# A new static order for a fused attention and feed-forward kernel, with Omega's transpose in steps, five buffers of attention outputs and constant matmuls in gaps

## Chip, cores and metric

The kernel runs on one core of one Trainium2 chip. The metric is device time in microseconds (us). Fast executions of one kernel mostly agree to within about 1% (three of the kernel before: 325.45 to 328.21 us). A run counts as slow when it is over 1.5% above the fastest of its kernel. A profiled span is some 1.7 us shorter than the time of the same run, in most runs (327.8 for 329.58 us before). The granted clock is the share of its full clock that the profile records for TensorE. In the profiles PE is TensorE, PEld its weight loads, DVE VectorE, ACT ScalarE, POOL GpSimd, SP SyncE; a q behind a name marks its instruction queue.

## What is computed

Eight batches of eight heads go through linear attention with random features. The 4608 rows that come out go through a two-layer feed-forward net.

```python
q_s, k_s = q * scale, k * scale            # q, k, v: (8, 8, 576, 64) float32
def phi(x):
    h = einsum('bhsd,md->bhsm', x, omega) - sum(x * x) / 2      # omega: (128, 64)
    return exp(h - max(h)) / sqrt(m)
kv, z = einsum('bhsm,bhsd->bhmd', phi(k_s), v), sum(phi(k_s), over s)
x = (phi(q_s) @ kv) / (phi(q_s) @ z + 1e-6)                      # -> (4608, 512)
h = x @ w_in                                                     # (512, 2048)
out = (h * sigmoid(1.702 * h)) @ w_out                           # (2048, 512), float32 out
```

## The kernel before

The work is cut into 32 attention items (item p is one pair of heads; four items are one batch) and eight blocks (one batch of 576 rows each through both layers). A block's first layer needs the attention outputs of its four items, transposed. In the steady loop from block 2 on, items of later batches are woven between the wide matmuls of the current blocks. Ahead of the loop stands a prologue: items 0 to 13, block 0's two layers, and block 1's first layer. Its steps are listed by hand, one call per step. That list is each engine's program order.

The output of an item is divided into a buffer `xb`, and a DMA transpose moves it to its place in `xt`, which the first layer reads. `xb` comes from a pool of three:

```python
work = ctx.enter_context(tc.tile_pool(name="work", bufs=3))
...
def xb_tile(p):
    if (p, "xb") not in st:
        st[p, "xb"] = work.tile([128, NCH, 128], BF16, name="xb", tag="xb")
    return st[p, "xb"]
...
def xt_dma(p):                                   # two pieces, on SyncE's queue
    xb = st.pop((p, "xb"))
    ...
    nc.sync.dma_start_transpose(dst[:, 0:512]..., xb[:, 0:4, :]...)
    nc.sync.dma_start_transpose(dst[:, 512:S], xb[64:128, 4, :])
```

The start, and two places of the hand-made list (`tk`, `tq`: PE transposes of k and q; `pk`, `pq`: projections; `e_..`: ScalarE exponentials; `halves_max`, `maxima`, `inverse`: VectorE; `scale_v`: values scaled, on GpSimd if True; `kv`, `nd`: the attention products; `mm1`, `mm2`: the wide matmuls of the two layers):

```python
warm_ps = bank("b1", [128, 512], F32, "warm_ps")
for _ in range(9):                               # constants, to bring the full clock
    nc.tensor.matmul(warm_ps[:], lhsT=warm[:, 0:128], rhs=warm[:])
...
def omega_T():
    for i in range(2):
        nc.vector.tensor_copy(out=om_b[:, 64 * i : 64 * i + 64], in_=om_f[:])
    omt_ps = bank("b1", [128, 128], BF16, "omt_ps")
    nc.tensor.transpose(omt_ps[:], om_b[:], ident[:])
    nc.vector.tensor_copy(out=omT2[:], in_=omt_ps[:])
...
    omega_T()
    load_k(0, 2, 3)
    k0_cast(False)                               # VectorE's part of the first k, behind Omega's copy
    k0_cast(True)
    tk_pe(0, "b0")
    ...                                          # cut
    xt_dma(6)
    pk_pe(9)
    ...
    nd2_pe(7, "qp")
    nd2_inv(7)
    nd2_div(7)                                   # needs a fourth xb while three wait for their transposes
    e_k5(9)
    ...
    xt_dma(7)
```

The softmax here doesn't subtract the row's maximum and nothing guards it: scores larger than these inputs give would overflow.

Of the kernel before, what the change touches and what calls it, by code (L numbers as in the profile page):

```python
# [13 lines left out]
F32 = mybir.dt.float32  # L14
# [7 lines left out]
def kernel(  # L22
# [45 lines left out]
    work = ctx.enter_context(tc.tile_pool(name="work", bufs=3))  # L68
    small = ctx.enter_context(tc.tile_pool(name="small", bufs=4))
# [19 lines left out]
    warm_ps = bank("b1", [128, 512], F32, "warm_ps")  # L89
    for _ in range(9):  # L90
        nc.tensor.matmul(warm_ps[:], lhsT=warm[:, 0:128], rhs=warm[:])  # L91
# [353 lines left out]
    def xb_tile(p):  # L445
        if (p, "xb") not in st:
            st[p, "xb"] = work.tile([128, NCH, 128], BF16, name="xb", tag="xb")
        return st[p, "xb"]
# [207 lines left out]
    om_f = const.tile([128, D], F32, name="om_f")  # L656
# [3 lines left out]
    nc.scalar.dma_start(om_f[:], omega[:, :])  # L660
# [7 lines left out]
    def omega_T():  # L668
        for i in range(2):
            nc.vector.tensor_copy(out=om_b[:, 64 * i : 64 * i + 64], in_=om_f[:])  # L670
        omt_ps = bank("b1", [128, 128], BF16, "omt_ps")
        nc.tensor.transpose(omt_ps[:], om_b[:], ident[:])
        nc.vector.tensor_copy(out=omT2[:], in_=omt_ps[:])
# [18 lines left out]
    with tc.manual_schedule(engines={ET.DVE, ET.Activation}):  # L692
        make_identity(nc, ident[:])
        omega_T()
        load_k(0, 2, 3)
        k0_cast(False)
        k0_cast(True)
        tk_pe(0, "b0")
        load_k(0, 1, 2)
        tk_cp(0, False)  # L700
        load_k(0, 3, 4)
        load_q(0, 1, 2)
        q0_cast(True)
        tk_pe(2, "b1")
        tk_cp(2, False)
        pf_pe(0)
        e_k5(0)
        load_q(0, 2, 3)
        pk_pe(0)
        e_km(0)  # L710
        tk_pe(1, "b0")
        q0_cast(False)
        tk_cp(1, False)
        tq_pe(0, "b1")
        tq_cp(0, True)
        halves_max(0)
        pf_pe(1)
        pk_pe(1)
        maxima(0)
        pq_pe(0)  # L720
        inverse(0)
        tk_pe(3, "b1")
        e_k5(1)
        tk_cp(3, False)
        tq_pe(1, "b0")
        load_v(0, 0, 1, nc.gpsimd)
        tq_cp(1, False)
        pr_pe(0)
        load_k(1, 0, 1)
        load_k(1, 1, 2)  # L730
        load_v(0, 1, 2, nc.gpsimd)
        e_km(1)
        load_k(1, 2, 3)
        halves_max(1)
        pk_pe(2)
        maxima(1)
        pf_pe(3)
        tq_pe(2, "b1")
        e_qm(0)
        pf_pe(2)  # L740
        inverse(1)
        load_v(0, 2, 4, nc.gpsimd)
        tq_cp(2, False)
        load_q(0, 3, 4)
        load_q(1, 0, 1)
        scale_v(0, True)
        pq_pe(1)
        tk_pe(4, "b0")
        e_km(2)
        pk_pe(3)  # L750
        tk_cp(4, False)
        e_k5(2)
        halves_max(2)
        kv_pe(0)
        e_qm(1)
        kv_cp(0)
        e_qr(0)
        maxima(2)
        nd_pe(0, 0, "b0")
        nd_inv(0, 0)  # L760
        load_win(0)
        e_k5(3)
        nd_pe(0, 1, "b1")
        nd_inv(0, 1)
        tk_pe(6, "qp")
        pr_pe(1)
        e_km(3)
        tk_cp(6, False)
        pr_pe(2)
        nd_div(0, 1, True)  # L770
        pf_pe(4)
        scale_v(1, True)
        halves_max(3)
        inverse(2)
        maxima(3)
        kv_pe(1)
        nd_div(0, 0, True)
        e_qr(1)
        xt_dma(0)
        load_q(1, 2, 3)  # L780
        pq_pe(2)
        e_qm(2)
        tk_pe(5, "b1")
        load_win(1)
        tk_cp(5, False)
        pk_pe(4)
        scale_v(2, True)
        e_k5(4)
        inverse(3)
        kv_cp(1)  # L790
        tq_pe(3, "b0")
        tq_cp(3, False)
        scale_v(3, True)
        tq_pe(4, "qp")
        tq_cp(4, False)
        load_k(2, 0, 1)
        e_qr(2)
        load_win(2)
        nd_pe(1, 1, "b0")
        nd_inv(1, 1)  # L800
        nd_pe(1, 0, "b1")
        nd_inv(1, 0)
        nd_div(1, 1, False)
        e_km(4)
        kv_pe(2)
        pf_pe(6)
        pq_pe(3)
        nd_div(1, 0, False)
        pk_pe(5)
        kv_cp(2)  # L810
        nd_pe(2, 1, "b0")
        nd_pe(2, 0, "b1")
        e_qm(3)
        nd_inv(2, 1)
        nd_inv(2, 0)
        kv_pe(3)
        pr_pe(3)
        nd_div(2, 0, False)
        xt_pe(1, "qp")
        pf_pe(5)  # L820
        nd_div(2, 1, True)
        xt_cp(1, False, S2, S)
        e_km(5)
        e_qr(3)
        xt_cp(1, False, 0, S2)
        kv_cp(3)
        xt_pe(2, "b1")
        tq_pe(6, "b0")
        xt_cp(2, False, S2, S)
        e_k5(5)  # L830
        xt_cp(2, False, 0, S2)
        pq_pe(4)
        tq_cp(6, False)
        e_k5(6)
        pk_pe(6)
        e_km(6)
        load_v(1, 0, 2, nc.gpsimd)
        nd_pe(3, 0, "b1")
        nd_pe(3, 1, "b0")
        nd_inv(3, 0)  # L840
        homes[0, 2] = "xx+"
        mm1(0, 2, 0, 1)
        nd_inv(3, 1)
        mm1(0, 2, 1, 2)
        nd_div(3, 0, False)
        nd_div(3, 1, False)
        homes[0, 1] = "xx"
        mm1(0, 1, 0, 1)
        mm1(0, 1, 1, 2)
        mm1(0, 2, 2, 3)  # L850
        halves_max(6)
        e_qm(4)
        homes[0, 3] = "b1"
        mm1(0, 3, 0, 1)
        xt_pe(3, "b0")
        xt_cp(3, False, 0, S2)
        xt_cp(3, False, S2, S)
        halves_max(5)
        maxima(5)
        homes[0, 0] = "kp"  # L860
        mm1(0, 0, 0, 1)
        halves_max(4)
        load_win(3)
        mm1(0, 0, 1, 2)
        mm1(0, 3, 1, 2)
        mm1(0, 3, 2, 3)
        load_k(1, 3, 4)
        homes[0, 6] = "qp+"
        mm1(0, 6)
        mm1(0, 2, 3, 4)  # L870
        maxima(4)
        load_q(1, 1, 2)
        homes[0, 5] = "b0"
        mm1(0, 5)
        homes[0, 7] = "qp"
        mm1(0, 7)
        homes[0, 8] = "kp+"
        mm1(0, 8)
        maxima(6)
        gelu_th(0, 5)  # L880
        gelu_mul(0, 5)
        inverse(4)
        load_q(1, 3, 4)
        load_q(2, 0, 1)
        gelu_th(0, 7)
        gelu_th(0, 2)
        gelu_mul(0, 2)
        gelu_th(0, 8)
        load_v(1, 2, 4, nc.gpsimd)
        gelu_mul(0, 8)  # L890
        homes[0, 11] = "b0"
        mm1(0, 11)
        gelu_th(0, 6)
        gelu_mul(0, 6)
        mm1(0, 1, 2, 3)
        mm1(0, 0, 2, 3)
        mm1(0, 1, 3, 4)
        load_k(2, 1, 2)
        inverse(5)
        mm1(0, 3, 3, 4)  # L900
        gelu_th(0, 1)
        gelu_mul(0, 1)
        homes[0, 10] = "xx+"
        mm1(0, 10)
        homes[0, 14] = "kp+"
        mm1(0, 14)
        gelu_th(0, 3)
        gelu_mul(0, 3)
        gelu_th(0, 11)
        gelu_mul(0, 11)  # L910
        gelu_th(0, 10)
        gelu_mul(0, 10)
        mm1(0, 0, 3, 4)
        gelu_th(0, 14)
        gelu_mul(0, 7)
        homes[0, 13] = "xx"
        mm1(0, 13)
        gelu_mul(0, 14)
        gelu_th(0, 0)
        load_wout(0)  # L920
        tk_pe(7, "b0")
        gelu_mul(0, 0)
        gelu_th(0, 13)
        homes[0, 12] = "qp+"
        mm1(0, 12)
        tk_cp(7, True)
        gelu_mul(0, 13)
        scale_v(5, True)
        load_wout(1)
        tk_pe(8, "b1")  # L930
        homes[0, 15] = "qp"
        mm1(0, 15)
        pk_pe(7)
        pf_pe(7)
        gelu_th(0, 12)
        tk_cp(8, True)
        gelu_th(0, 15)
        scale_v(4, True)
        pr_pe(4)
        gelu_mul(0, 12)  # L940
        kv_pe(4)
        inverse(6)
        kv_cp(4)
        e_km(7)
        load_wout(2)
        gelu_mul(0, 15)
        tq_pe(5, "b0")
        homes[0, 4] = "b1"
        mm1(0, 4)
        tq_cp(5, False)  # L950
        tk_pe(9, "qp")
        e_qr(4)
        gelu_th(0, 4)
        e_k5(7)
        tq_pe(7, "b0")
        tq_cp(7, False)
        gelu_mul(0, 4)
        load_wout(3)
        tk_cp(9, False)
        halves_max(7)  # L960
        homes[0, 9] = "kp+"
        mm1(0, 9)
        gelu_th(0, 9)
        scale_v(6, True)
        gelu_mul(0, 9)
        mm2_mms(0, 2, 0, "b0")
        pq_pe(5)
        pf_pe(8)
        kv_pe(5)
        pr_pe(5)  # L970
        load_q(2, 2, 3)
        tq_pe(8, "b1")
        nd2_pe(4, "kp")
        nd2_inv(4)
        tq_cp(8, False)
        load_q(2, 3, 4)
        kv_cp(5)
        nd2_div(4)
        e_qm(5)
        mm2_mms(0, 2, 1, "b0")  # L980
        e_k5(8)
        e_qr(5)
        pq_pe(6)
        load_v(2, 0, 2, nc.gpsimd)
        pr_pe(6)
        kv_pe(6)
        pr_pe(7)
        e_qr(6)
        pk_pe(8)
        load_q(2, 1, 2)  # L990
        load_k(2, 3, 4)
        mm2_mms(0, 1, 0, "b1")
        e_qr(7)
        maxima(7)
        inverse(7)
        kv_cp(6)
        e_qm(6)
        xt_dma(4)
        nd2_pe(5, "xx")
        nd2_inv(5)  # L1000
        nd2_div(5)
        xt_dma(5)
        e_km(8)
        halves_max(8)
# [303 lines left out]
```

## Time and profile before

| | before |
|---|---|
| time, median of 3 (range) | 327.63 us (325.45 to 328.21) |
| profiled span | 327.8 us |
| loop's first second-layer matmul starts | 90.39 us |
| first wide matmul; dense from | 26.80; 28.48 us |
| TensorE at half clock (granted clock 0.50) | 20.1 to 23.3 and 61.0 to 67.6 us |

The profile of the kernel before is of a run of its own, which took 329.58 us, 2.0 us above the median. All positions and stage times below are of that run.

Here are two parts of the page of the kernel before: busy time of TensorE with its share of the span, and then the span in 40 slices of 8.2 us. In the slices a digit is tenths of busy time (9 is 90% or more) or, for PEclk, tenths of the full clock.

```profile
PE 314.5 (96%) x2637; PEld 168.5 (51%) x2637; DVE 196.7 (60%) x383; ACT 188.9 (58%) x363; POOL 83.6 (25%) x152
...
PE   7979999699989999999999999999999999999995
PEclk9979999789999999999999999999999999999999
DMA  8999999959579778995898579951213011001031
```

From the thirteenth slice on TensorE is full. What can be won lies in the slices before: its digits dip in the first, the third and the eighth, its clock in the third, eighth and ninth, and the DMA stands at 9 through nearly all of the same stretch. A clock digit is an average over 8 us, so stretches of half clock show as a 7 or an 8.

The timeline of the kernel before, in the columns start, duration, engine, line, operation and (in brackets) idle time before it: ScalarE's first big exponential, SyncE's issue of item 0's transpose, and TensorE's first wide matmuls.

```profile
8.53 1.02 ACT L362 ACTIVATE ke<-pk 128x1024 bf16<-128x1024 f32 x1
...
18.51 1.30 SPq L511 DMA_TRANSPOSE xt<-xb  x1
...
26.80 1.46 PE L547 MATMUL ph<-xt,win 128*128 128x512 bf16 x6 [0.73 <-ACT ke L362]
...
28.48 1.89 PE L547 MATMUL ph<-xt,win 128*128 128x512 bf16 x8
```

Item 0's transpose landed 8.2 us after its issue, at 26.7 us, and the first wide matmul followed at 26.80. The wait is named after an exponential there, which ended 0.1 us after the transpose landed.

Next, the windows view of the kernel before. Its columns are the stretch, its length, busy time (and instructions) of PE, PEld, DVE, ACT and POOL, and then the granted clock, the DMA share and GB/s.

```profile
56.00:58.00 2.00, 1.37 (x15) 0.84 (x13) 0.00 (x0) 0.97 (x4) 2.00 (x5) 1.00 1.41 120
58.00:60.00 2.00, 0.61 (x8) 0.48 (x9) 1.55 (x3) 0.57 (x2) 0.23 (x1) 1.00 1.23 204
60.00:62.00 2.00, 1.03 (x14) 0.43 (x12) 1.81 (x5) 0.96 (x1) 0.00 (x0) 0.75 1.21 230
62.00:64.00 2.00, 1.94 (x29) 1.51 (x29) 0.00 (x1) 0.70 (x4) 0.00 (x0) 0.50 0.97 180
```

TensorE idles 3 us between 56 and 62 us and is then "full", but at half clock: four 512-column matmuls take 1.91 us at 63.76 us, against 1.03 us at 59.64. By the granted clock of 0.50, about half of those busy microseconds are lost too (an estimate). VectorE did nothing in 56 to 58. The chain that ended last says why (start, duration, what):

```profile
46.23 0.73 DVE xb L486
...
48.24 10.05 DMA xt<-xb
...
58.42 0.82 DVE xb L486
...
61.66 0.36 DVE qT L193
...
62.06 0.61 PE pq L286 x2
```

The second piece of item 4's output was transposed in 10.05 us by a DMA. Item 7's division (58.42) waited for its buffer. A copy of q behind that division held up a projection, and so TensorE. In the waits view the same is "DVE xb <- DMA xt<-xb: 3.9" us for VectorE, and for TensorE (total, times, longest):

```profile
PE tq L213 <- DVE xb L486: 2.0, 1, 2.0
PE pq L286 <- DVE qT L193: 1.0, 1, 1.0
PE ph L547 <- DVE gT L571: 0.9, 1, 0.9
```

### The profile page before, as it was taken

How to read it: one execution, taken by the hardware profiler on the slowest of the kernel's cores; microseconds unless marked ns; L12 is line 12 of the kernel's file. 1: busy time of each engine (PE TensorE's matmuls, PEld its weight loads, DVE VectorE, ACT ScalarE, POOL GpSimd, SP SyncE). 2: the span in 40 equal slices, each digit the busy share in tenths (PEclk: the TensorE clock that was granted, in tenths of full speed). 3: DMA queues.
4: the chain of work that ended last, by engine and by line, in shares of the span. 5: the costliest groups of instructions: out<-in, count | busy, mean ns of one | idle time of the engine just before them, and what ended most of it. 6: DMA issues, size and time to landing. Idle time of an engine off the chain costs nothing.

```text
span 327.8 us, 6655 instructions
## 1 busy us (share of the span) xinstructions
PE 314.5 (96%) x2637; PEld 168.5 (51%) x2637; DVE 196.7 (60%) x383; ACT 188.9 (58%) x363; POOL 83.6 (25%) x152
## 2 busy tenths in 40 slices
PE   7979999699989999999999999999999999999995
PEld 3664555355545555555555555555555444444444
DVE  2868973478956766666666666666665443344300
ACT  2985976477736666666666666666664444434411
POOL 8693585110151116111611061000101010001100
PEclk9979999789999999999999999999999999999999
DMA  8999999959579778995898579951213011001031
GB/s 176 259 131 228 250 212 242 189 140 183 111 145 254 129 126 229 170 144 110 224 174 145 110 195 171 176 112 50 52 50 68 35 47 50 32 32 35 32 90 70
DMA packets 61614, 44.09 MB, mean 135 GB/s; under 512 B 46033, under 2 KB 54608, under 8 KB 61264
## 3 DMA queue, kind: packets, MB, share of 16 engines
q0 software_dynamic: 13552, 24.55, 36.0%
q1 hardware_dynamic: 47888, 19.10, 31.0%
q8 instruction: 20, 0.33, 0.4%
q14 instruction: 10, 0.08, 0.1%
q10 hardware_dynamic: 144, 0.03, 0.0%
HBM read 37.39 MB, written 15.66 MB: 162 GB/s over the span
## 4 chain that ended last, share of the span: by engine, by line
PE 83%; DVE 7%; DMA 5%; ACT 2%; issue 1%; SPq 1%; DVEq 0%; ACTq 0%
PE ph L547 35%; PE po L587 34%; DMA xt<-xb 3%; PE xx L228 3%; PE pk L271 3%; PE nd L443 2%; DMA vst<-in_v_dram 2%; PE pq L286 2%; DVE gT L571 2%; PE warm_ps L91 1%; DVE maxE L397 1%; PE tk L200 1%; PE po L624 1%; ACT xb L463 1%; DVE xb L486 1%
## 5 line engine op out<-in xcount | busy, mean ns | idle before, releaser
L547 PE MATMUL ph<-xt,win 128*128 128x512 bf16 x576 | 144.6, 379 | 1.6 <-DVE gT L571 0.9
L587 PE MATMUL po<-wout,gT 128*128 128x512 bf16 x560 | 142.4, 381 | 0.0
L563 ACT ACTIVATE th<-ph 128x512 bf16<-128x512 f32 x144 | 85.9, 605 | 95.8 <-PE ph L547 95.6
L571 DVE SCALAR_TENSOR_TENSOR gT<-th,ph 128x512 bf16<-128x512 bf16 x144 | 96.8, 682 | 62.9 <-ACT th L563 62.8
L547 PEld LDWEIGHTS <-win 128*128 128x128 bf16 x576 | 63.0, 114 | 57.0 <-issue 2.5
L587 PEld LDWEIGHTS <-gT 128*128 128x128 bf16 x560 | 52.7, 98 | 59.6 <-issue 1.0
L610 POOL DMA_DIRECT2D out_dram<-osb x44 | 23.5, 537 | 175.4 <-ACT osb L600 169.2
L362 ACT ACTIVATE ke<-pk 128x1024 bf16<-128x1024 f32 x32 | 33.0, 1030 | 5.0 <-PE pk L271 4.8
L374 ACT ACTIVATE qe<-pq 128x1024 bf16<-128x1024 f32 x32 | 33.1, 1034 | 3.2 <-PE pq L286 3.2
L600 ACT ACTIVATE osb<-po 128x512 f32<-128x512 f32 x34 | 20.4, 599 | 16.3 <-PE po L587 16.3
L392 DVE TENSOR_TENSOR half<-ke 128x576 bf16<-128x576 bf16 x32 | 15.0, 469 | 23.7 <-ACT ke L371 23.7
L486 DVE TENSOR_TENSOR xb<-nd,rden 128x640 bf16<-128x640 f32 x28 | 23.1, 823 | 4.8 <-DMA xt<-xb 3.9
L397 DVE TENSOR_REDUCE maxE<-half 128x9 f32<-128x576 bf16 x32 | 24.0, 753 | 0.9
L408 POOL TENSOR_TENSOR vp<-vst,emax 128x576 bf16<-128x576 f32 x11 | 12.6, 1149 | 41.0 <-DVE emax L401 29.4
L443 PEld LDWEIGHTS <-qe 128*128 128x128 bf16 x320 | 14.3, 100 | 7.3 <-issue 1.1
L228 PE MATMUL xx<-vp,ke 64*128 64x65 bf16 x576 | 16.8, 197 | 0.5 <-DVE vp L414 0.5
L408 DVE TENSOR_TENSOR vp<-vst,emax 128x576 bf16<-128x576 f32 x21 | 15.9, 758 | 2.2 <-DMA vst<-in_v_dram 1.3
L443 PE MATMUL nd<-kvs,qe 128*128 128x65 bf16 x320 | 15.7, 197 | 0.4 <-ACT kvs L245 0.4
L228 PEld LDWEIGHTS <-ke 64*128 64x128 bf16 x576 | 13.9, 99 | 1.8 <-issue 0.9
L271 PEld LDWEIGHTS <-qk 64*128 64x128 bf16 x180 | 7.6, 118 | 9.9 <-issue 7.8
L371 ACT ACTIVATE ke<-xx 128x128 bf16<-128x128 f32 x32 | 9.3, 296 | 4.8 <-PE xx L271 4.4
L245 ACT ACTIVATE kvs<-xx 128x130 bf16<-128x130 f32 x32 | 9.7, 303 | 2.9 <-PE xx L228 1.5
(61 smaller groups left out, 192.1 us busy)
## 6 DMA issues: line engine op xcount, KB each, us to landing
vst<-in_v_dram SPq DMA_DIRECT2D x5, 1152.0 KB, 9.4
out_dram<-osb POOLq DMA_DIRECT2D x12, 256.0 KB, 2.3
sk<-in_k_dram POOLq DMA_DIRECT2D x19, 160.0 KB, 7.7
vst<-in_v_dram POOLq DMA_DIRECT2D x5, 576.0 KB, 9.6
sq<-in_q_dram POOLq DMA_DIRECT2D x20, 144.0 KB, 8.2
win<-in_moe_w_in_dram POOLq DMA_DIRECT2D x4, 512.0 KB, 8.8
wout<-in_moe_w_out_dram POOLq DMA_DIRECT2D x4, 512.0 KB, 8.7
out_dram<-osb POOLq DMA_DIRECT2D x10, 192.0 KB, 3.2
```

What stands on the lines that cost most here:

```text
L228: yield lambda t=t: nc.tensor.matmul(kv[:, i, :], lhsT=ke[lo : lo + 64, t, :], rhs=vp[lo : lo + 64, t, :], start=(t == 0), stop=(t == KT - 1),
L362: nc.scalar.activation(out=ke_tile(p)[:, 0:8, :].rearrange("p (c s) f -> p s c f", s=2), in_=st.pop((p, "pk"))[:].rearrange("p s (c f) -> ...
L374: nc.scalar.activation(out=qe_tile(p)[:, :, :, 0:256], in_=st.pop((p, "pq"))[:].rearrange("p s (i r) -> p s i r", i=2), func=AF.Exp, scale ...
L397: nc.vector.reduce_max(out=maxE[:], in_=st.pop((p, "half"))[:], axis=AX.X)
L408: eng.tensor_tensor(out=vp[:, :, 0:64], in0=tiles[b]["v"][:, c, :].rearrange("p (t d) -> p t d", d=D), in1=emax[:].unsqueeze(2).to_broadca ...
L443: nc.tensor.matmul(nd[:, t, :], lhsT=st[p, "qe"][:, i, c0 : c0 + 128], rhs=st[p, "kvs"][:, i, :])
L486: nc.vector.tensor_tensor(out=xb_tile(p)[:].rearrange("p t (i d) -> p i t d", i=2), in0=nd[:, :, :, 0:64], in1=st.pop((p, "rden2"))[:].uns ...
L547: mm = nc.tensor.matmul(ph, lhsT=win[f // 4][:, c, f % 4 : 512 : 4], rhs=xt[c][:, i * TB : (i + 1) * TB], start=(c == 0), stop=(c == CM - 1),)
L563: act = nc.scalar.activation(out=th[:], in_=ph_tile(i, f), func=AF.Tanh, scale=0.851)
L571: dve = nc.vector.scalar_tensor_tensor(out=gTs[i][:, f, :], in0=th[:], scalar=1.0, in1=ph_tile(i, f), op0=ALU.add, op1=ALU.mult)
L587: nc.tensor.matmul(pos[i, r][:], lhsT=gTs[i][:, f, r * 128 : (r + 1) * 128], rhs=wout[:, f, :], start=(f == 0), stop=(f == NFC - 1),)
L610: eng.dma_start(out[row : row + (n - 1) * step + 1 : step, :], osb[p0 : p0 + n, :])
```

## The change

The intent: start sooner, let no output wait for a buffer, keep the clock up with matmuls of constants where the array has nothing to do, and use a new static order of the whole prologue that matches these. The order is most of the diff (some 500 lines); what it does is told by the calls shown. TensorE gets ten instructions more: two of the nine constants at the start are removed, and twelve are added in gaps. What is computed stays the same, though a few operations move between engines. Block 0's second layer now ends before block 1's first layer starts. In the old order its last part was interleaved with block 1.

```diff
+    xbp = ctx.enter_context(tc.tile_pool(name="xbs", bufs=5))
...
-    warm_ps = bank("b1", [128, 512], F32, "warm_ps")
-    for _ in range(9):
-        nc.tensor.matmul(warm_ps[:], lhsT=warm[:, 0:128], rhs=warm[:])
...
-            st[p, "xb"] = work.tile([128, NCH, 128], BF16, name="xb", tag="xb")
+            st[p, "xb"] = xbp.tile([128, NCH, 128], BF16, name="xb", tag="xb")
...
-    nc.scalar.dma_start(om_f[:], omega[:, :])
+    nc.scalar.dma_start(om_f[:], bass.AP(omega.tensor, 0, [[D, M_F], [0, 2], [1, D]]))
...
-    def omega_T():                              # (cut: cast, transpose and copy in one)
+    def om_cast(on_act):
+        copy(on_act, om_b[:].rearrange("p (i d) -> p i d", i=2), om_f[:])
+    def om_pe(home): ...
+    def om_cp(on_act): ...
+    def warm_mm(n, cols, home):
+        t = bank(home, [128, 512 if home[0] == "b" else 1024], F32, "warm_ps")
+        for _ in range(n):
+            nc.tensor.matmul(t[:, 0:cols], lhsT=warm[:, 0:128], rhs=warm[:, 0:cols])
...
-        omega_T()
-        load_k(0, 2, 3)
-        k0_cast(False)
-        k0_cast(True)
-        tk_pe(0, "b0")
+        load_k(0, 2, 3)
+        k0_cast(True)
+        load_k(0, 1, 2)
+        k0_cast(False)
+        make_identity(nc, ident[:])
+        warm_mm(7, 512, "qp")
+        tk_pe(0, "xx")
+        q0_cast(True)
+        load_q(0, 1, 2)
+        om_cast(False)
+        om_pe("b0")
+        q0_cast(False)
+        warm_mm(3, 128, "qp")
+        tq_pe(0, "b1")
...                                              (the rest of the order, and 5 more warm_mm calls)
```

## The prediction

> **What bounds it now.** From 92 us to the end TensorE is full (windows view: 10.00 of 10.00 us) in rounds of 8.3 us. The change does not touch that loop, whose first matmul starts at 90.4 us (timeline). What can be won lies before. That prologue's matmuls, counted warm, are about 65 us (192 wide ones at 216 ns start to start, 42 us; 14 attention items at about 1.6 us), so about 25 us are lost:
> - 0 to 27 us: casts, then a chain of ScalarE exponentials (1.03 us each; ScalarE is 1.5 to 2.0 us busy of each 2 us from 8 us on). The first wide matmul, at 26.8 us, also needs item 0's DMA transpose (issued 18.5, 8 us to land); they are dense from 28.5 us.
> - TensorE at half rate: eight 128-column matmuls take 0.71 us until about 12.3 us, 0.40 us after; slow again at 20.1 to 23.3 and 61.0 to 67.6 us, where the granted clock is 0.50. [...]
> - 57.4 to 59.4 and 61.0 to 62.1 us: TensorE idle. The chain of waits shows why: the fourth attention output has no buffer among three until a DMA transpose of 10 us lands; VectorE waits 3.9 us for it. With the half clock after it this costs about 6 us, the largest single loss.
> - 82 and 91 us: 0.5 and 0.9 us of waits.
>
> **What the change does.** (1) Five output buffers: the 3.9 us wait goes; with it 3 us of idle TensorE and 3 us of half clock. (2) Startup: the cast of k no longer stands behind Omega's transpose (6.07 us now, about 3.8 then); seven constant matmuls instead of nine (0.43 us each). First projection near 6.1 instead of 7.8 us. (3) Constant matmuls in gaps: hidden if the gap is real, 0.3 to 0.9 us where not; they may bring the full clock earlier. (4) New order: two key exponentials and one query exponential fewer before the wide matmuls, but 1.3 us of TensorE work moves behind with them. Item 0's transpose issues perhaps 1.3 us earlier; ScalarE's chain still sets that. The second matmul of block 0 now ends before block 1's first matmuls, so block 1 packs 16 Gelus with the last exponentials: about 18 us of ScalarE work in 17.5 us of TensorE work.
>
> **Critical path.** Gain 6 us (buffers) + 1 to 2 us (start); lost again: 1 us waiting for item 7's transpose (6 to 10 us each now), 1 us ScalarE or VectorE limit in block 1, perhaps 1 us of half clock at the first wide matmuls. Net about 5 us: loop starts near 85.5 us; 322.5 us, 8 in 10 within 318 to 326. Chances: faster by over 2% 0.35, within 2% 0.64, slower 0.01.
>
> **What would show it.** No wait of VectorE's output division for a DMA; no granted clock of 0.5 near 61 us; first exponential near 6.9 us (8.1 now); wide matmuls dense near 26.5 us; rounds still 8.3 us and 237 us from loop start to end.
>
> **What would make it wrong.** Weight loads or batch 1's values landing late, as the DMA queues are nearly full until 69 us (new stalls of several us); a cold array through the first wide matmuls (up to 3 us); or a new order without new waits, which would give 8 us or more.

6 us, and 1 to 2 us, less the three losses of about 1 us each, come to "about 5 us". "Warm" and "cold" are full and half clock (0.40 and 0.71 us for eight 128-column matmuls). The "up to 3 us" for a cold array is the author's estimate; the trace before has some 3 us lost to half clock after 61 us.

## The result

| | before | after |
|---|---|---|
| time, median (range) of 4 runs | 327.92 us (325.45 to 333.16) | 318.76 us (318.28 to 319.03) |
| profiled span | 327.8 us | 317.0 us |
| first big exponential | 8.53 us | 6.81 us |
| first wide matmul; dense from | 26.80; 28.48 us | 21.42; 22.90 us |
| item 0's transpose: issued; landed after | 18.51; 8.2 us | 16.35; 4.9 us |
| loop's first second-layer matmul | 90.39 us | 80.45 us |
| from there to the end | 237.4 us | 236.6 us |

The ratio of the times is 0.9749, with a 95% interval of 0.9702 to 0.9796: faster. The run of 333.16 us counts as slow. A ratio here compares one kernel's fast runs with the other's fast runs of the same rounds, so it is not quite the ratio of the medians. All kernels below gave the right result.

The same lines of the page, of the kernel after:

```profile
PE 309.5 (98%) x2647; PEld 165.2 (52%) x2647; DVE 197.4 (62%) x379; ACT 189.0 (60%) x364; POOL 86.1 (27%) x154
...
PE   8889999999999999999999999999999999999995
PEclk9999999999999999999999999999999999999999
DMA  8999999998798679775979395911122100001121
```

TensorE is at 9 from the fourth slice on. Its clock reads 9 everywhere, and the DMA is as full as before. The timeline of the kernel after: the first big exponential, the issue of item 0's transpose, the first wide matmuls, and the loop's start:

```profile
6.81 1.02 ACT L360 ACTIVATE ke<-pk 128x1024 bf16<-128x1024 f32 x1
...
16.35 1.29 SPq L509 DMA_TRANSPOSE xt<-xb  x1
...
21.42 0.81 PE L545 MATMUL ph<-xt,win 128*128 128x512 bf16 x3 [0.21 <-DMA xt<-xb]
...
22.90 7.07 PE L545 MATMUL ph<-xt,win 128*128 128x512 bf16 x32
...
80.45 1.03 PE L585 MATMUL po<-wout,gT 128*128 128x512 bf16 x4
```

The windows of the kernel after:

```profile
60.00:62.00 2.00, 2.00 (x46) 1.24 (x43) 1.05 (x2) 1.71 (x3) 2.00 (x3) 1.00 1.15 106
62.00:64.00 2.00, 2.00 (x21) 1.19 (x18) 0.55 (x2) 2.00 (x6) 1.36 (x4) 1.00 1.27 257
64.00:66.00 2.00, 2.00 (x11) 0.91 (x8) 1.97 (x4) 1.88 (x3) 0.00 (x0) 1.00 1.20 185
```

And TensorE's waits in the whole execution after, longest in total first:

```profile
PE warm_ps L681 <- DVE warm L89: 1.5, 1, 1.5
PE nd L441 <- ACT xb L461: 0.6, 2, 0.4
PE nd L441 <- DVE qT L191: 0.4, 1, 0.4
PE xx L226 <- POOL vp L412: 0.4, 1, 0.4
PE ph L545 <- DMA xt<-xb: 0.2, 1, 0.2
```

Only the wait for the first constant's data, at the very start, is longer than 0.6 us. VectorE waits for no DMA in the division.

The profiled gain is 10.8 us, and most of it can be accounted for by stage. From 56 to 70 us TensorE was idle 3.05 us before (10.95 busy of 14.00) and 0 after. In the half clock at 61.0 to 67.6 us it was busy for 5.57 us, and by the clock of 0.50 half of that, an estimated 2.8 us, is lost as well. Together that is 5.8 us. Between 70 and 92 us TensorE idled 1.1 us before (waiting for scaled values at 82 us and for a Gelu at 91 us) and 0 after. About 3.9 us are left for the start: TensorE idled 5.3 us of the first 28 before and 3.9 after, the half clock at 20.1 to 23.3 us cost 1.6 us (estimated likewise), and 0.9 us is not broken down.

This profiled gain is larger than the timed one, which is about 8.2 us (0.0251 of 328), because the profiled run before was a slow one among the fast. How much half clock the kernel before meets differs between its executions. The record has the mean granted clock of its 44 executions in the rounds of the experiments, slow ones included: the 23 with less than 0.985 took 328.2 us on average (the profiled run has 0.983), the 8 with 0.992 or more took 326.1, and the single one with 1.000 took 325.39. So the half clock goes with some 2 us of time from run to run, and the kernel after, in other rounds, is still about 7 us faster than executions that hardly met it.

### The profile page after: what moved, and what is told of

It is laid out like the page before. It is cut to its first block, busy times and chain, and to the rows that moved or that the text cites. A ratio compares the mean times of both kernels' runs of the same rounds, so it can differ in the third digit from the quotient of the medians.

```text
span 317.0 us, 6672 instructions
## 1 busy us (share of the span) xinstructions
PE 309.5 (98%) x2647; PEld 165.2 (52%) x2647; DVE 197.4 (62%) x379; ACT 189.0 (60%) x364; POOL 86.1 (27%) x154
## 4 chain that ended last, share of the span: by engine, by line
PE 93%; DVE 3%; DMA 2%; ACT 0%; issue 0%; ACTq 0%; DVEq 0%
PE ph L545 40%; PE po L585 38%; PE xx L226 3%; PE nd L441 3%; PE pk L269 3%; PE pq L284 2%; DMA xt<-xb 2%; PE po L622 1%; PE warm_ps L681 1%; DVE half L390 1%; PE tk L198 1%; PE tq L211 1%; DVE maxE L395 1%; DVE qT L191 0%; DVE kT L191 0%; PE xx L284 0%
## 5 line engine op out<-in xcount | busy, mean ns | idle before, releaser
L390 DVE TENSOR_TENSOR half<-ke 128x576 bf16<-128x576 bf16 x32 | 16.8, 524 | 26.8 <-ACT ke L369 23.6
L406 POOL TENSOR_TENSOR vp<-vst,emax 128x576 bf16<-128x576 f32 x12 | 14.2, 1179 | 27.8 <-DVE emax L399 16.3
L226 PE MATMUL xx<-vp,ke 64*128 64x65 bf16 x576 | 15.8, 191 | 0.5 <-POOL vp L412 0.4
L406 DVE TENSOR_TENSOR vp<-vst,emax 128x576 bf16<-128x576 f32 x20 | 15.1, 757 | 0.8
L226 PEld LDWEIGHTS <-ke 64*128 64x128 bf16 x576 | 13.1, 95 | 2.1 <-issue 1.3
L160 POOL DMA_DIRECT2D sk<-in_k_dram x20 | 10.9, 544 | 0.0
L174 POOL DMA_DIRECT2D sq<-in_q_dram x20 | 10.4, 518 | 0.0
```

The costliest lines, as they stand in the source:

```text
L226: yield lambda t=t: nc.tensor.matmul(kv[:, i, :], lhsT=ke[lo : lo + 64, t, :], rhs=vp[lo : lo + 64, t, :], start=(t == 0), stop=(t == KT - 1),
L406: eng.tensor_tensor(out=vp[:, :, 0:64], in0=tiles[b]["v"][:, c, :].rearrange("p (t d) -> p t d", d=D), in1=emax[:].unsqueeze(2).to_broadca ...
```

## The experiments

Twelve kernels were run. Names that begin with b are built from the kernel before, names with a from the kernel after. "Before" in the measured lines is the kernel before in the same rounds. The kernel after was not in these rounds: where a ratio is held against its 0.9749, the two come from different rounds.

### b_bufs5: five buffers, old order

```diff
+    xbp = ctx.enter_context(tc.tile_pool(name="xbs", bufs=5))
-            st[p, "xb"] = work.tile(...)
+            st[p, "xb"] = xbp.tile(...)
```

> The old order with the output buffers as a pool of their own, five instead of three; nothing else. Theory A (the missing buffer is the cause of both the idle and the half clock at 57 to 68 us): no wait of VectorE's output division for a DMA, no idle TensorE at 57 us, full clock through 61 to 68 us, span about 6 us shorter, ratio near 0.98. Theory B (the DMA queues are the limit; the wait only moves to the transpose of item 7): the first wide matmul of block 1 waits for a DMA transpose instead, gain under 2 us.

Measured: fast runs 326.9 to 330.93 us, two slow runs of 333 us, ratio to before 1.0064 (1.0016 to 1.0113): no gain, slightly slower. VectorE's wait did go, and TensorE is busy 3.95 of the 4 us from 56 to 60 us. Then comes this (the longest wait of TensorE in b_bufs5, and two windows of it):

```profile
PE ph L548 <- DMA xt<-xb: 4.1, 1, 4.1
```

```profile
60.00:62.00 2.00, 1.63 (x32) 0.89 (x31) 1.93 (x5) 1.83 (x3) 0.00 (x0) 1.00 1.85 87
62.00:64.00 2.00, 0.00 (x0) 0.00 (x0) 0.21 (x1) 0.27 (x1) 1.31 (x2) 1.00 1.16 132
64.00:66.00 2.00, 0.28 (x1) 0.11 (x1) 0.00 (x0) 0.00 (x0) 0.00 (x0) 0.61 1.16 181
```

TensorE has 4.1 us of nothing at 61.6 to 65.7 us, waiting for the transpose itself, and then the half clock. The chain that ended last has one piece for it:

```profile
54.95 10.73 DMA xt<-xb
65.68 0.04 issue
65.72 2.29 PE ph L548 x5
```

Item 7's transpose was issued earlier than in the kernel before (54.95 against 59.27 us), but took 10.7 instead of 6.6 us. The buffer was not what the stage waited for. Its wait was the first of two on the same slow transposes.

### b_fill: constant matmuls at the two waits, old order

```diff
+        warm_mm(9, 512, "xx")
         tq_pe(9, "qp")
...
+        warm_mm(4, 512, "b0")
         pq_pe(9)
```

> The old order and the old three buffers, with 9 and 4 constant matmuls put into the two gaps of TensorE at 57 and 61 us. The wait for the buffer stays. If the half clock after the gap is a cost of its own (about 3 us of matmuls at half rate), the granted clock stays 1.00 and the span shortens by about 3 us. If the clock does not matter there, because VectorE or a DMA limits that stretch anyway, under 1 us.

Measured: median 326.3 us, ratio 0.999 (0.9949 to 1.0031). The clock stays at 1.00 from 56 to 70 us in its profile (it is 0.50 at 18.1 to 21.5 us), the wait of the division for the buffer remains, and the loop starts at 87.73 us, 2.7 us sooner than before, in a profiled run of 327.29 us. But 1.5 us of these 2.7 come from the start, which the edit does not touch. The timeline of b_fill shows item 0's transpose and the first wide matmul:

```profile
16.35 1.34 SPq L511 DMA_TRANSPOSE xt<-xb  x1
...
25.29 1.48 PE L547 MATMUL ph<-xt,win 128*128 128x512 bf16 x5 [1.44 <-DMA xt<-xb]
```

The transpose is issued at 16.35 us, not 18.51, although all instructions up to there are those of the kernel before. What the two profiles show to differ is TensorE's clock: here eight 128-column matmuls take 0.45 us at 7.04 and 0.40 at 8.60 us, in the kernel before still 0.71 us at 9.73. So some 2 us of the old start depend on when the full clock comes in that execution; it came after 12 us in three of the four profiles with old start and old order, and by 8.2 us in all profiles that have the new start or the new order, with constants at the start. The timed gain of b_fill is not resolved: keeping the clock through a gap of waiting is worth 1.7 us at most here (the interval's lower end).

### a_bufs3 and a_bufs4: fewer buffers, new order

```diff
-    xbp = ctx.enter_context(tc.tile_pool(name="xbs", bufs=5))
+    xbp = ctx.enter_context(tc.tile_pool(name="xbs", bufs=3))     # a_bufs4: 4
```

> The new order with three output buffers. If the new order needs the five: item 3's division at 21.4 us must wait for item 0's second DMA transpose (landing near 24.4 us), so the wide matmuls get dense about 2 to 3 us later; 2 to 3 us longer than the new kernel. If the new order alone removed the wait, under 0.5 us.

> The new order with four output buffers: item 3 has a buffer of its own, and item 7's division at 55.5 us waits for nothing older than item 3. Expected within 0.5 us of the new kernel. If it is slower by 1 us or more, the fifth buffer does work of its own.

Measured: three buffers 322.25 us, ratio 0.9863 (0.9823 to 0.9903); four buffers 319.69 us, 0.9787 (0.9752 to 0.9823). The interval of three buffers lies above that of the kernel after, so in the new order the buffers are worth about 1.1% (0.9863 less 0.9749). In the profiled run with three buffers TensorE waits 1.7 us for a division (tk <- DVE xb), a wait that the kernel after does not have. A fifth buffer against four is not resolved. The same edit that costs a little in the old order gains in the new one.

### b_start and a_startold: the start alone, and the order without it

```diff
 b_start (the kernel before, with the new start):
-        omega_T()  ...  k0_cast(False)  k0_cast(True)  tk_pe(0, "b0")
+        k0_cast(True)  k0_cast(False)  warm_mm(7, 512, "b1")  ...  tk_pe(0, "b0")
+        om_cast(False)  om_pe("b1")  om_cp(False)
 a_startold (the kernel after, Omega in one piece ahead of k's cast, 9 constants; removed lines cut):
+        warm_mm(9, 512, "qp")  om_cast(False)  om_pe("b0")  om_cp(False)
+        k0_cast(True)  k0_cast(False)  tk_pe(0, "xx")
```

> The old order with the new start alone: cast of k first, seven constant matmuls, Omega's transpose in steps behind k's. First exponential about 1.3 us earlier. If the old order passes that on, the wide matmuls begin 1 to 1.5 us earlier and the span shortens by as much; if the old order's later waits absorb it (the loads of k, q arrive no earlier, ScalarE's order), under 0.5 us.

> The new order with Omega's transpose in one piece ahead of the cast of k, behind nine constant matmuls, as in the old kernel. First large exponential about 1.5 us later (8.3 instead of 6.8 us). If the start is on the chain to the first wide matmuls, the span grows by 1 to 1.5 us; if slack is taken up by the waits before the wide matmuls (a DMA transpose, ScalarE), by under 0.5 us.

Measured: b_start 326.36 us, ratio 1.0005 (0.9954 to 1.0056); a_startold 321.39 us, ratio 0.9833 (0.9781 to 0.9885). The new start put into the old order gains nothing. Taken out of the new order it gives back some 2.7 us (0.9833 less 0.9749, times 328), though the two intervals overlap. The profile of b_start is of the slowest of its six runs (330.30 us), so it can't tell where the lead goes in a usual run. In it the first exponential is at 6.39 us and item 0's transpose is issued at 16.31 us, as early as in the kernel after (and as in b_fill, with the old start), but it lands 8.7 us later instead of 4.9. The first wide matmul is still 1.7 us sooner than before (25.11 for 26.80); half clock at 26.0 to 29.4 and 60.1 to 63.5 us, a wait of 2.9 us for a division at 60.2 us and one of 1.9 us for a transpose at 69.1 us follow. The longest wait of TensorE in b_start in total, and the timeline of its first wide matmuls:

```profile
PE ph L544 <- DMA xt<-xb: 4.0, 2, 2.1
```

```profile
25.11 1.89 PE L544 MATMUL ph<-xt,win 128*128 128x512 bf16 x5 [2.08 <-DMA xt<-xb]
27.32 4.87 PE L544 MATMUL ph<-xt,win 128*128 128x512 bf16 x17
```

In the old order two weight loads of 512 KB were issued 4.0 and 1.3 us before this transpose (in b_start). In the new order one was issued 5.9 us before it and the next one 0.4 us after it. There is scatter in this time: b_bufs5, whose loads are issued as in the kernel before, has 6.3 us for 8.2. In the profiles of fast runs it is 4.1 to 6.1 us in the new order (seven profiles) and 6.3 to 8.8 in the old (five).

In a_startold the first big exponential is at 8.04 us, 1.2 us later than in the kernel after, but the first wide matmul only 0.4 us later (21.79 for 21.42). The waits that its profile has and the kernel after has not are later: 1.0 us for a transpose of outputs at 63.8 us and 1.5 us for one of q at 72.4 us.

### a_nogap and a_nowarm: without the gap constants, without any constants

```diff
 a_nogap:  -  warm_mm(3, 128, "qp"), (2, 512, "b0"), (3, 128, "b0"), (3, 128, "b1"), (1, 512, "b1")
 a_nowarm: -  warm_mm(7, 512, "qp"), and the five calls of a_nogap as well
```

> The new order without the five groups of constant matmuls in the gaps (12 in all); the seven at the start stay. If they carry the clock: the full clock comes later than the 6.2 us of the new kernel or is lost near 15 to 20 us, matmuls at half rate there, 1 to 3 us longer. If the seven at the start and the denser order suffice: within 0.5 us, or a little faster since the gaps' matmuls no longer stand ahead of others.

> The new order without the seven wide constant matmuls at the start (those in the gaps stay). TensorE is then nearly unused until 4.5 us, so the full clock should come at 9 to 13 us instead of 6.2 us. If TensorE's latency at half clock is on the chain of the start, 1 to 2 us longer; if ScalarE's exponentials set the pace whatever the clock, under 0.5 us.

The edit of a_nowarm that ran is not the one announced: its kernel has no constants at all, neither the seven at the start nor the twelve in the gaps.

Measured: a_nogap 319.31 us, ratio 0.977 (0.9734 to 0.9807); fast runs as quick as the kernel after. One of its six runs took 326.33 us, and it happens to be the profiled one: its clock is 0.50 at 11.5 to 18.3, 25.1 to 28.5 and 69.5 to 72.9 us, with 4.2 us of waits for transposes. The four runs after lie within 0.75 us. So the gap constants buy no time in a usual run that these runs resolve. Whether they prevent the rare slow one is suggested by this single run, not shown. a_nowarm: 321.41 us, ratio 0.9846 (0.9794 to 0.9897), one run of 325.29 us (the profiled one, which counts as slow). All nineteen together are worth some 3 us in the fast runs (0.9846 less 0.9749), with intervals that just overlap. Against a_nogap, in the same rounds, the first seven are worth 2.5 us (0.9846 less 0.977), again with intervals that just overlap. In the profile eight 128-column matmuls run at half speed until after 15 us (in the kernel after they take 0.40 us from 7.9 us on), later than the 9 to 13 us estimated for the announced edit, and item 0's transpose is issued at 18.26 us, as late as in the kernel before.

### b_casts: 600 KB of copies moved out of the transposes' way, old order and five buffers

```diff
-        cast_k(3, 3, 4)   cast_q(3, 2, 3)   cast_q(3, 3, 4)   cast_k(3, 2, 3)    # each in its place
         scale_v(10, True)
+        cast_k(3, 3, 4)   cast_q(3, 2, 3)   cast_q(3, 3, 4)   cast_k(3, 2, 3)
```

> The old order with five output buffers, as in the run with five buffers alone, and four of the eight casts of batch 3 moved behind item 10's scaling of v on the GpSimd queue (issue near 62 instead of 54 to 57 us). Theory B (the DMA queues set when item 7's transpose lands: 10.7 us when seven casts are issued around it): it lands 6 to 7 us after its issue at 55 us, so near 62 us; the 4.1 us wait of block 1's first matmul falls under 1 us and no half clock follows; 4 to 6 us shorter than five buffers alone, ratio to the old kernel near 0.987. If the casts do not matter, the wait stays at about 4 us and the ratio at 1.006.

Measured: 327.12 us, ratio 0.9996 (0.9946 to 1.0047), against 1.0064 for five buffers with the copies in place: about 2 us, with overlapping intervals. The profiled run was the slowest of its six (330.29 us) and still waited 4.6 us for transposes (1.1 us at block 0's start, 3.4 at block 1's); those of items 4 to 7 took 9.4 to 12.6 us. Moving these copies alone does not mend the old order. It is a miss for the simple form of the theory that counts kilobytes, as far as one slow profile tells.

### a_win2early: a second weight load ahead of item 0's transpose, new order

```diff
         load_win(0)
+        load_win(2)
         pr_pe(2)
...
-        load_win(2)
```

> The new order with the second weight load issued right behind the first, at about 11.3 us instead of 16.8 us, so that it is on the queues before item 0's transpose (issued 16.4 us). If what stands on the queues sets the landing time (4.9 us here, 8.2 to 8.7 us in the old orders, where a weight load was issued 1.3 to 2.3 us earlier): the load has 5 us of head start here, so the landing may even come sooner, 4 to 5.5 us, as most of it has drained; if any outstanding weight load delays it, 7 to 8 us and the first wide matmul 2 us later. Span within 0.7 us in the first case, 1.5 to 2.5 us longer in the second.

Measured: 320.95 us, ratio 0.979 (0.9747 to 0.9834). GpSimd issues the load before it scales item 0's values, so these came about 1.3 us later (TensorE waited 1.1 us for them) and the transpose was issued at 17.99 instead of 16.35 us. It then landed in 4.1 us: the load had some 6 us to drain. The profile also has half clock at 14.2 to 17.6 us, right behind that wait of TensorE, which the kernel after has not. So the loss began at the issuing engine and not in the queue, and this run says little about the queue.

### a_dve1: item 1's values scaled on VectorE

```diff
-        scale_v(1, True)
+        scale_v(1, False)                          # and placed right behind kv_pe(0)
```

> The new order with item 1's scaling of v on VectorE (0.94 us there) instead of GpSimd. In the new kernel VectorE's maximum of item 2's halves, normally 0.45 us, lasts 2.1 us (11.8 to 13.9 us) while GpSimd scales v of items 0 and 1 (11.2 to 14.0 us). If GpSimd's work blocks VectorE's, that maximum ends about 1.2 us earlier, near 12.7 us, the second half of item 0's numerators (waiting for VectorE until 14.4 us) starts near 13.5 us, and item 0's transpose is issued 0.3 to 0.8 us earlier; span 0.3 to 0.8 us shorter, faster than both kernels. If the long maximum has another cause, it stays long and VectorE's chain grows by 0.9 us: 0.5 us longer.

In the kernel after, one VectorE maximum of 0.45 us takes 2.14 us while GpSimd scales values beside it:

```profile
11.82 2.14 DVE L390 TENSOR_TENSOR half<-ke 128x576 bf16<-128x576 bf16 x1
...
11.24 1.17 POOL L406 TENSOR_TENSOR vp<-vst,emax 128x576 bf16<-128x576 f32 x1
12.50 1.14 POOL L406 TENSOR_TENSOR vp<-vst,emax 128x576 bf16<-128x576 f32 x1
```

The maximum overlaps two scalings and ends 0.3 us after the second. Measured: 321.16 us, ratio 0.9794 (0.9742 to 0.9846). The maximum shrank to 1.06 us as expected (it overlaps one scaling there, 11.38 to 12.55 us, and again ends 0.3 us after it), but item 0's transpose was issued only 0.2 us sooner, and landed 6.1 us later. The long maximum does lie on the kernel after's chain of work that ended last (2.06 us at 11.91). With it shortened, TensorE waited 0.8 us for scaled values instead of 0.4, and half clock followed at 22.7 to 26.1 us. So this maximum does take longer beside scalings on GpSimd (0.45 us with none, 1.06 with one, 2.14 with two), and taking one away in this way gained nothing; what a shorter maximum is worth by itself stays open.

### a_extra: one useless load of 576 KB at 50 us, new order

```diff
+    extra = const.tile([128, 2, KT * D], F32, name="extra")
...
+        nc.gpsimd.dma_start(extra[:], nine(v, 2, 0, 2))
         cast_q(3, 2, 3)
```

> The changed kernel with one useless load added: half of batch 2's values (576 KB) into a tile that nobody reads, issued on the GpSimd queue just ahead of the first cast copy of batch 3 that stands behind batch 2's last q load, near 50.1 us, after item 4's transposes and before those of items 6 and 7. No compute instruction is added; all outputs stay right. Theory Q (a transpose lands when what was issued ahead of it has drained, and the new order gains because it has about 0.5 to 0.7 MB less outstanding at this point): at about 0.22 MB per us the 0.59 MB delay the transposes of items 6 and 7 by 2 to 4 us (to land after 9 to 11 us instead of 5.2 to 8.1), block 1's first matmul (62.2 us, no wait now) waits 2 to 4 us for a DMA xt<-xb, and the span grows by 2 to 5 us (ratio to the kernel before near 0.985 to 0.99 instead of 0.975). If also 1 us or more of half clock follows, it is the upper end. Rival R (the order of matmuls and exponentials alone gives the gain and the DMA has slack there): no wait at block 1's first matmul above 0.5 us, ratio 0.972 to 0.978.

Measured: 321.8 us, ratio 0.9812 (0.976 to 0.9863). Its median is 3.0 us above that of the kernel after, but the ratio lies between what the two theories expected and its interval reaches into both, so the profile has to decide. The profiled span grew from 317.0 to 320.4 us. Item 6's transpose landed after 11.3 instead of 8.1 us, and item 7's after 9.2 instead of 6.2 us, 3 us later each, as theory Q had it. Two waits of TensorE in a_extra, and the timeline at the first matmuls of blocks 0 and 1:

```profile
PE ph L546 <- ACT osb L599: 2.7, 1, 2.7
PE ph L546 <- DMA xt<-xb: 0.8, 1, 0.8
```

```profile
22.02 0.81 PE L546 MATMUL ph<-xt,win 128*128 128x512 bf16 x3 [0.84 <-DMA xt<-xb]
...
64.82 0.60 ACT L599 ACTIVATE osb<-po 128x512 f32<-128x512 f32 x1 [2.91 <-DMA out_dram<-osb]
...
65.47 1.33 PE L546 MATMUL ph<-xt,win 128*128 128x512 bf16 x4 [2.74 <-ACT osb L599]
```

Block 1's first matmul started at 65.47 instead of 62.18 us. Most of that wait is named after ScalarE's copy of an earlier output, and the line of ScalarE shows that this copy had waited 2.9 us for a DMA: an output store that was issued at 54.1 us and took 10.6 us. So the added load held up the stores as well as the transposes. The wait of 0.8 us is not its doing: it stands at block 0's first matmul, 28 us before the load is issued, and is scatter of item 0's transpose (5.6 us for 4.9). Of the 3.4 us of span 0.6 come from there and 2.7 from block 1's start. Rival R, which expected no wait above 0.5 us, falls in the profile. The DMA queue is on the edge of the critical path at block 1's start: the new order has no slack of 600 KB there.

## Why the prediction was right, and where its size was off

The range (318 to 326 us) holds the result, 318.76 us. The chance of faster by over 2% was put at 0.35 only; 0.64 was on a change within 2%, so the likelier class did not come. Against the centre of 322.5 us the gain was undersized by 3.7 us. Point by point:

- **The loop is untouched, and all gain lies before it: right.** It runs 236.6 us from its start to the end after and 237.4 before. The difference is the 0.9 us wait at 91 us, which the prediction listed but did not count.
- **"Gain 6 us (buffers)": the size was right by luck, the cause wrong.** The idle time and half clock from 56 to 70 us, 5.8 us in this pair of profiles, did go. But b_bufs5 shows that five buffers take away the named wait and win none of the time. The wait moved to the next reader of the same transposes (4.1 us, then half clock). The step that failed is "the 3.9 us wait goes; with it 3 us of idle TensorE and 3 us of half clock". A chain that names a buffer names the first thing to be held up by a slow transfer; the transfer itself took 10.05 us. In the new order the same piece of item 4 lands after 5.2 us, and item 7's is issued at 56.50 instead of 59.27 us. The new order also puts work into the wait: before block 1's first layer it runs all 64 second-layer matmuls of block 0, where the old order had run 48. At the 0.86 us that four take in the chain, the other 16 are an estimated 3.4 us, nearly as long as the wait of 4.1 us in b_bufs5. No run separates the two.
- **"+ 1 to 2 us (start)": too small.** The first big exponential was predicted right (6.81 for "near 6.9"; it was the big one that came there, while the 8.1 quoted beside it was a small one's). The wide matmuls were dense from 22.90 us, not "near 26.5". The term that was mis-sized is item 0's transpose. It was expected to be issued 1.3 us earlier and, by what follows from the numbers, to take about as long as before; it was issued 2.2 us earlier and took 4.9 instead of 8.2. The stage gained about 3.9 us in this pair of profiles. The 2.2 us hold for this pair alone: b_fill issued it at 16.35 us with the old start, once the full clock came early. With the issue as early, b_fill and b_start still start the wide matmuls near 25 us, because the transpose takes 8.7 to 8.8 us there.
- **"Lost again: 1 us ..., 1 us ..., perhaps 1 us of half clock": none of it came.** Block 1's first matmul waits for nothing, ScalarE is 15.8 us busy of the 18 us from 62 to 80 us while TensorE is full, and the clock never falls once it is full, near 6.5 us. This is what the prediction's last clause named, "a new order without new waits, which would give 8 us or more".
- **Constants in gaps: "hidden if the gap is real": right.** a_nogap's fast runs are as quick.
- **The half clock.** The traces show that TensorE starts at half clock and gets the full one later: in the kernel before eight 128-column matmuls still take 0.71 us at 9.7 us and 0.40 us at 14.1 us; in the kernel after they take 0.55 us at 6.2 us and 0.40 us at 7.9 us. They do not show after how much work it comes: in the kernel before TensorE is busy with constants for 4.0 us from 1.46 us on, and half clock lasts until after 12 us; in b_fill, with the same start, it has ended by 8.6 us.

**What is shown and what stays open.** Shown: no part alone brings anything that these runs resolve (buffers +0.6%, start 0.0%, fillers -0.1%, these at other places than the change's), while the whole brings -2.5%. Taking buffers, start or all constants from the whole costs 0.8 to 1.1%, across rounds; of these only the buffers' interval is clear of the kernel after's. Shown by the profiles: the quicker transpose of item 4 goes with the order, and with none of the other parts by itself. Its first piece takes 5.0 to 5.6 us in all nine profiles with the new order, whatever was taken out, and 9.6 to 11.8 us in all five with the old. Item 6's is no quicker (8.1 us after, 5.8 before). Shown in one profile: in the new order, DMA traffic added at 50 us makes stores and transposes land 3 us later and turns into a wait of 2.7 us at block 1's start. A reading why, which fits but is not proved: the new order issues loads sooner and stands 0.5 to 0.6 MB ahead (12.6 against 12.1 MB moved by 56 us, 7.95 against 7.32 by 36 us), so less is outstanding when transposes are issued. At item 4's issue the loads still under way sum to about 1.6 MB of destination in the kernel after and 2.4 MB before. In both, the first piece of that transpose lands with or just after a load of values issued ahead of it (both at 57.25 us, within 3 ns, before; 52.7 after 52.2 us in the kernel after). Why they land together is not shown; no run here isolates it. b_casts, where fewer bytes did not shorten the transposes, says that bytes alone are not the rule. The new order with the old start and three buffers was not run, so what the order is worth by itself is open. Subtracting the parts from the whole does not tell it, because their effects do not add up.

No experiment beats the kernel after.

## What to carry to other kernels

A wait for a buffer that a transfer holds is a wait for the transfer (3.9 us for the buffer before, 4.1 us for a transpose in b_bufs5): before adding buffers, ask who reads what the transfer brings and when, because that reader will wait next. When several edits each remove one of two waits in series, test them singly and together; alone each may show nothing (here +0.6%, 0.0% and -0.1% singly, -2.5% the whole). Where the DMA queues are full, a load can delay the small transfers issued behind it (a_extra: 576 KB, 3 us), so read landing times from the profile before and after, and try to issue weights that are needed late behind the transfer that is needed soon; no run here tests that step by itself. Before a profile is explained, compare several of the same code: the start of b_fill and of the kernel before are the same instructions, and item 0's transpose is issued 2.2 us apart.

## What else was measured

- A small transpose among loads: the same 128 x 512 piece took from 2.4 us (kernel after, issued at 77.6 us) to 12.6 us (b_casts, at 53.7 us) from issue to landing in the prologue.
- Where the clock fell: at 20.1 us although TensorE was busy 2.26 of the 4.0 us before that and never idle for more than 0.7 us at once, and at 61.0 us with 1.98 us busy of 4.0 and one gap of 2.0 us. That makes no rule: in a_bufs3 TensorE was busy 2.26 us from 20 to 24 us too, and the clock stayed at 1.00.
- The granted clock of the profile reads 1.00 in the first 12 us of the kernel before, while 512-column matmuls there run at 0.43 us each, half the speed of those at 28.48 us (0.216 us start to start). So the record misses this slow start.
- VectorE beside GpSimd: in the kernel after a maximum of 128 x 576 bf16 values that takes 0.45 us at 9.76 us takes, at 11.82 us, 2.14 us beside two GpSimd scalings.
